# A scan, a routed mixture of experts and a gated block in one kernel: another order of the scan's round, and a tile of its own for the experts' row numbers

## The chip, the cores and the metric

The kernel runs on one core of one Trainium2 chip. The metric is the time of one execution in device microseconds. Before the change the median of three runs is 994.81 us (993.85 to 996.44).

## The reference

Three layers follow each other. The first is linear attention with a decay gate, for 4 batches of 8 heads, 768 steps and 48 columns:

```python
for t in range(S):
    state = f[:, :, t, :, None] * state + np.einsum('bhd,bhe->bhde', k[:, :, t], v[:, :, t])
    y[:, :, t] = np.einsum('bhd,bhde->bhe', q[:, :, t], state)
```

Its output is taken as 3072 tokens of 384 numbers. Each token goes to one of 8 experts, the one of the largest cosine logit; the result is weighted with that expert's softmax probability:

```python
for e in range(E):
    mask = expert_idx == e
    h = np.maximum(x[mask] @ w1[e], 0.0)
    out[mask] = gate_w[mask, None] * (h @ w2[e])
```

with w1[e] of 384x1024 and w2[e] of 1024x384. The last layer is `(x @ w_a) * (x @ w_b) @ w_out`, with 1536 hidden columns. All tensors are fp32. Big products are made as three fp32r matmuls of a high and a low part of each operand.

## The kernel before, in words

The order of every engine's work is written out by hand (`manual_schedule`): each engine runs its instructions in the order in which the program issues them, and waits on semaphores where data or a buffer is not ready. DMAs are issued from the SP queue, in order too, apart from the gathers and scatters, which POOL issues.

**Scan.** The 768 steps are cut into 6 chunks of 128; chunk and batch make 24 groups (`NG`), and the loop over `g` does one group a round. For a group, `scan_b` runs a backward product of the gates on VectorE (tile `Bt`, L188), POOL scales the keys with it (`kt`, L191), and column 0 of `Bt`, the decay over the chunk, goes through a POOL operation into `al_all` (L193). `scan_r` runs the forward scan (`Rt`, L200), `q_scale` scales the queries (L208). `scores` (L244) makes the 128x128 products, evacuated in two halves: VectorE multiplies one by a mask (L261), ScalarE copies the other (L251) and POOL zeroes its upper triangle (L252). `inter` (L268) adds the contribution of the state, `intra` (L275) that of the chunk. `turn_k` and `u_part` make the group's addition to the state, `s_add` (L296) adds it on VectorE, and `s_scale` (L216 on ScalarE for three head pairs, L218 on VectorE for the fourth) multiplies the state by `al_all`. `turn_y` (L302) turns the output into token rows, with the logits beside them. Work is pipelined over rounds: in round `g` the scans are of group `g+2`, scores and masks of `g+1`, outputs of `g`, rows of `g-1`. `warm_up` in each round puts three or one matmul without use on TensorE (L307).

**Routing.** When a set of groups is done (`ROUNDS`), `route` picks experts and positions in small VectorE steps that `tick` deals out between the round's other work, ranks tokens with small matmuls (`rk`), and `scatter_row` lets POOL scatter 128 token rows at a time into `slots` in DRAM (L422), two a round. Each row carries the token's number in column 0 and the gate in column 1.

**Experts.** Expert `e` has 448 places. `rows_load` (L752) reads its 448 rows of 388 numbers from `slots` into the one tile `rows`, 112 partitions of 4 rows; `rows_gate` (L761, ScalarE) multiplies one of the four by the gates, `x_turn` (L781, L784, L785) transposes a third of the columns and splits it. `ids_store` (L769) writes column 0 of `rows`, the token numbers, to a list in DRAM; it has to land before `rows` is loaded anew. The loop runs 64 steps `s`, 8 steps `j` for each expert: `h_part` makes 128 hidden columns (L788 to L790; relu L810 on ScalarE, low part L811 on VectorE), `y_part` of the step before adds them to three outputs (L841), which step 0 of the next expert copies out (L859, L857). `w_more` handles weight pieces of 768 KB with two buffers `raw`: SP loads one (L683), ScalarE makes the high part (L689), POOL and VectorE the low part (L692); a piece of the last layer's weights takes three steps, with four VectorE operations on it (L700 to L710).

In step `j` of expert `e` the program has, after `h_part` and `w_more`: the turn of `e+1` at 3 to 5; at 5 the store of `e+1`'s numbers and the load of `e+2`'s rows; the first gate of `e+2` at 7 and the other three at 0 to 2 of the next expert:

```python
            if 3 <= j <= 5:
                x_turn(e + 1, j - 3)
            elif j == 7:
                rows_gate(e + 2, 0)
            elif j < 3:
                rows_gate(e + 1, j + 1)
            if j == 5 and e + 1 < NE:
                ids_store(e + 1)
                rows_load(e + 2)
            y_part(s - 1)
```

**Last layer.** 6 tiles of 512 tokens by 12 steps of 18 + 12 matmuls, then a scatter to the output.

Of the kernel before, what the change touches and what calls it, by code (L numbers as in the profile page):

```python
# [18 lines left out]
L = 128  # L19
# [15 lines left out]
RB = 8  # L35
# [7 lines left out]
ROUNDS = (7, 15, 19, 21, 23)  # L43
C0 = 2.0 ** -15
NWARM3 = 24
NKEEP = (3, 1)


def build(tc, I, out, dbg=None):
# [50 lines left out]
    def w_hi():  # L100
        n = wstate["hi"]
        if n < wstate["load"]:
            wstate["hi"] += 1
            A.activation(out=w_tile(n)[:, 0], in_=RAW[n], func=ACTF.Copy)

    def w_lo(eng, parts=3):
        n, at = divmod(wstate["lo"], 3)
        if n >= wstate["hi"]:
            return
# [7 lines left out]
    with tc.manual_schedule():  # L117
# [32 lines left out]
        qkf_t = [ob_p.tile([QP, 3, NP, L], F32, name=f"qkf{i}") for i in range(NQ)]  # L150
        u_full = ps_u.tile([128, NP, HP], F32, name="u_ps")
# [31 lines left out]
        def scan_b(g):  # L183
# [3 lines left out]
            Bt = at_p.tile([QP, NP, L + 1], F32, tag="Bt", name="Bt", bufs=2)  # L187
# [5 lines left out]
            G.tensor_scalar(out=al_all[:, g], in0=Bt[:, :, 0], scalar1=1e-30, scalar2=None, op0=ALU.max)  # L193
# [16 lines left out]
        def s_scale(g, a, b):  # L210
# [81 lines left out]
        def s_add(g):  # L292
            if g < 0 or g // B == NCH - 1:
                return
            Sb = S_t[g % B]
            V.tensor_tensor(out=Sb, in0=Sb, in1=u_ps, op=ALU.add)  # L296

        def turn_y(g):
            d = st[g]
            d["x"] = xt = ps_x.tile([128, NP, XW], F32, tag="x", name="x_ps")  # L300
# [13 lines left out]
        def x_sq(g, rd):  # L314
            i, xt = rd["n"], st[g]["x"]
            junk = x_p.tile([128, NP, 2 * D], BF16, tag="junk", name="junk", bufs=1)
# [10 lines left out]
        def x_lg(g, rd):  # L327
            V.tensor_reduce(out=rd["lg"][:, rd["n"]], in_=st[g]["x"][:, :, 2 * D:XW].rearrange("p a e -> p e a"),
                            axis=AX.X, op=ALU.add)

        def x_done(g, rd):
            st.pop(g)
            rd["n"] += 1
# [5 lines left out]
        def route(rd, i0):  # L339
# [6 lines left out]
            def until(k):  # L346
                while it[0] < i0 + k:
                    yield

            yield from until(0.5)  # L350
            nrm = rt("nrm", 1)
            G.tensor_tensor(out=nrm[:, :, 0], in0=ssq, in1=half[:, 0:nb], op=ALU.pow)
            mx = rt("mx", 1)
# [3 lines left out]
            V.tensor_tensor(out=eq, in0=lg, in1=bc(mx), op=ALU.is_ge)  # L357
            z = rt("z")
# [9 lines left out]
            yield from until(1)  # L368
# [9 lines left out]
            V.tensor_scalar(out=nrm, in0=nrm, scalar1=1e-6, scalar2=None, op0=ALU.add)  # L378
            yield
            V.reciprocal(out=nrm, in_=nrm)  # L380
            yield
            V.tensor_tensor(out=z, in0=z, in1=bc(nrm), op=ALU.mult)
            yield from until(1.5)
            A.activation(out=z, in_=z, func=ACTF.Tanh, scale=0.5)
# [10 lines left out]
            new = r_p.tile([128, NE], F32, tag="new", name="new")  # L395
            V.tensor_reduce(out=new, in_=oh.rearrange("p b e -> p e b"), axis=AX.X, op=ALU.add)
            yield
            V.tensor_tensor(out=run, in0=run, in1=new, op=ALU.add)
            yield
            yield from until(2)  # L400
# [13 lines left out]
            for i in range(nb):  # L414
                scaled.append((rd["xb"][:, i], posi[:, i]))

# [12 lines left out]
        def finish(n, upto=1000):  # L429
            it[0] = upto  # L430
            for r in bg[:n]:
# [779 lines left out]
```

## Time and profile before

| | |
|---|---|
| median of the three runs | 994.81 us |
| the profiled execution | 993.71 us, span 991.9 us |
| TensorE, weight load | busy 876.5 us (88%), 757.6 us (76%) |
| VectorE, ScalarE, POOL | busy 438.5, 347.6, 282.1 us |
| mean granted clock of TensorE | 0.927 |
| HBM read and written | 63.79 and 11.90 MB |

The page divides the span of 991.9 us among engines, lines and waits. Its line for TensorE in 40 slices of 24.8 us is `5898888888569578696876999989999999999996`, and that of its granted clock `7898798779798797978999999999999999999999`: 9 is full or nearly so, which of the clock's two levels a stretch has is read in finer windows. The scan lasts to about 180 us, the routing's last rounds and the reading of the first rows to 205, the experts to about 530, the last layer to the end. An engine's idle time counts only where the next one waits for it, so each stage is read by itself.

### The profile page before, as it was taken

To read this page: it belongs to the slowest core of one execution; us is meant where nothing else is said; L and a number is where in the kernel's file an instruction comes from. 1 tells how busy PE (TensorE), PEld (TensorE's weight loads), DVE (VectorE), ACT (ScalarE), POOL (GpSimd) and SP (SyncE) were. 2 spreads that over 40 slices of the span, in tenths; PEclk is the share of its full clock that TensorE was granted. 3 is DMA by queue.
4 is the path that set the end of the run, shared out by engine and by line. 5 is a ranking of instruction groups with operands and counts; after the bars stand their busy time and mean duration, and the time that the engine had idled before them with its cause. 6 is when DMAs were issued, how large, how long until landed. Compare 5 with 4: busy or idle time off the path is not lost.

```text
span 991.9 us, 12790 instructions
## 1 busy us (share of the span) xinstructions
PE 876.5 (88%) x5055; PEld 757.6 (76%) x5060; DVE 438.5 (44%) x719; ACT 347.6 (35%) x631; POOL 282.1 (28%) x267
## 2 busy tenths in 40 slices
PE   5898888569578696876999989999999999999996
PEld 3686776359567595765898878888888888888886
DVE  8899798432324233231467883222222222222222
ACT  3586565323325243242543432122122122122111
POOL 7474766653133151423422322001001001001001
PEclk7898798779798797978999999999999999999999
DMA  9677653244243442434342320000000000000000
GB/s 174 161 185 174 168 141 97 89 120 128 62 124 108 111 128 62 130 120 123 99 94 96 98 95 26 7 1 25 9 1 24 9 1 23 11 1 18 15 1 35
DMA packets 39286, 76.58 MB, mean 77 GB/s; under 512 B 7180, under 2 KB 21348, under 8 KB 39220
## 3 DMA queue, kind: packets, MB, share of 16 engines
q1 hardware_dynamic: 36020, 65.91, 25.5%
q0 software_dynamic: 3072, 9.49, 2.6%
q8 instruction: 42, 0.69, 0.3%
q10 hardware_dynamic: 128, 0.30, 0.1%
q14 instruction: 24, 0.20, 0.1%
HBM read 63.79 MB, written 11.90 MB: 76 GB/s over the span
## 4 chain that ended last, share of the span: by engine, by line
issue 36%; PE 29%; DVE 15%; POOL 8%; DMA 8%; ACT 3%; SPq 0%; POOLq 0%; ACTq 0%; DVEq 0%
DMA raw<-moe_w 4%; PE pa L789 4%; PE pa L790 4%; PE pa L788 4%; PE po L841 4%; POOL w L692 3%; DVE Bt L188 2%; PE pq L963 2%; PE pq L961 2%; PE pq L962 2%; DMA idlist<-rows 2%; DVE Rt L200 2%; DVE gl L950 2%; PE ph L788 1%; PE ph L789 1%
## 5 line engine op out<-in xcount | busy, mean ns | idle before, releaser
L790 PE MATMUL pa<-a,w 128*128 128x512 f32 (+1 forms) x438 | 170.5, 389 | 0.0
L789 PE MATMUL pa<-a,w 128*128 128x512 f32 (+1 forms) x438 | 170.4, 389 | 0.0
L788 PE MATMUL pa<-a,w 128*128 128x512 f32 (+1 forms) x438 | 169.0, 386 | 0.0
L948 DVE TENSOR_TENSOR rows<-rows,pa 128x512 f32<-128x512 f32 (+1 forms) x73 | 49.6, 680 | 242.7 <-PE pa L790 226.6
L841 PE MATMUL po<-hh,w 128*128 128x448 f32 x384 | 100.1, 396 | 55.9 <-ACT hh L810 49.9
L975 POOL DMA_INDIRECT out<-yT,idx x24 | 23.4, 974 | 363.8 <-ACT yT L973 358.3
L841 PEld LDWEIGHTS po<-hh,w 128*128 128x128 f32 x384 | 74.1, 200 | 67.2 <-ACT hh L810 52.6
L811 DVE SCALAR_TENSOR_TENSOR hl<-ph,hh 128x448 fp32r<-128x448 f32 x64 | 39.8, 623 | 164.5 <-ACT hh L810 164.5
L692 POOL TENSOR_TENSOR w<-raw,w 128x512 fp32r<-128x512 f32 x56 | 84.9, 1538 | 60.6 <-ACT w L689 60.6
L944 ACT ACTIVATE rows<-pa 128x512 f32<-128x512 f32 (+1 forms) x73 | 43.1, 591 | 164.7 <-PE pa L790 164.4
L963 PE MATMUL pq<-w,gl 128*128 128x384 f32 x288 | 97.5, 339 | 2.8 <-DVE gl L950 2.7
L961 PE MATMUL pq<-w,gh 128*128 128x384 f32 x288 | 97.0, 337 | 0.8 <-ACT gh L949 0.8
L962 PE MATMUL pq<-w,gh 128*128 128x384 f32 x288 | 96.8, 336 | 0.4 <-POOL w L710 0.4
L949 ACT ACTIVATE gh<-rows 128x512 fp32r<-128x512 f32 (+1 forms) x73 | 45.6, 625 | 143.9 <-DVE rows L948 143.9
L790 PEld LDWEIGHTS pa<-a,w 128*128 128x128 f32 x438 | 82.2, 188 | 16.8
L710 POOL TENSOR_TENSOR w<-raw,w 128x768 fp32r<-128x768 f32 x18 | 33.9, 1882 | 212.1 <-ACT w L709 212.1
L789 PEld LDWEIGHTS pa<-a,w 128*128 128x128 f32 x438 | 82.2, 188 | 15.4
L788 PEld LDWEIGHTS pa<-a,w 128*128 128x128 f32 x438 | 82.3, 188 | 15.1
L950 DVE TENSOR_TENSOR gl<-rows,gh 128x512 fp32r<-128x512 f32 (+1 forms) x73 | 60.0, 822 | 52.1 <-ACT gh L949 49.3
L788 PE MATMUL ph<-a,w 128*128 128x448 f32 x192 | 73.7, 384 | 0.0
L789 PE MATMUL ph<-a,w 128*128 128x448 f32 x192 | 72.8, 379 | 0.0
L790 PE MATMUL ph<-a,w 128*128 128x448 f32 x192 | 72.4, 377 | 0.0
(169 smaller groups left out, 1433.6 us busy)
## 6 DMA issues: line engine op xcount, KB each, us to landing
raw<-moe_w SPq DMA_DIRECT2D x32, 768.0 KB, 4.7
qkf<-qkf SPq DMA_DIRECT2D x44, 288.0 KB, 5.2
rows<-slots SPq DMA_DIRECT2D x7, 679.0 KB, 6.3
vx<-vx SPq DMA_DIRECT2D x24, 192.0 KB, 2.5
raw<-moe_w_a SPq DMA_DIRECT2D x6, 768.0 KB, 7.7
raw<-moe_w_b SPq DMA_DIRECT2D x6, 768.0 KB, 4.6
raw<-moe_w_out SPq DMA_DIRECT2D x6, 768.0 KB, 4.5
slots<-raw SPq DMA_DIRECT2D x8, 291.0 KB
```

Of the source, the lines that this page charges most:

```text
L692: (G if i < NPOOL else V).tensor_tensor(out=wt[:, 1, f], in0=raw[:, f], in1=wt[:, 0, f].bitcast(F32), op=ALU.subtract)
L788: T.matmul(out=out, lhsT=wh, rhs=xh, start=first, stop=False)
L789: T.matmul(out=out, lhsT=wl, rhs=xh, start=False, stop=False)
L790: T.matmul(out=out, lhsT=wh, rhs=xl, start=False, stop=last)
L841: T.matmul(out=OS[e][k], lhsT=w[:, j % 4, k * 128:(k + 1) * 128], rhs=x, start=(j == 0 and w is wh and x is hh), stop=(j == FJ - 1 and x i ...
L944: A.activation(out=ab[:, r], in_=pa, func=ACTF.Copy)
L948: V.tensor_tensor(out=ab[:, r], in0=ab[:, r], in1=pp[1], op=ALU.mult)
L949: A.activation(out=gh[:, r], in_=ab[:, r], func=ACTF.Copy)
L950: V.tensor_tensor(out=gl[:, r], in0=ab[:, r], in1=gh[:, r].bitcast(F32), op=ALU.subtract)
L961: T.matmul(out=q, lhsT=gh[:, c], rhs=wh[:, f % 4], start=(f == 0), stop=False)
L962: T.matmul(out=q, lhsT=gh[:, c], rhs=wl[:, f % 4], start=False, stop=False)
L963: T.matmul(out=q, lhsT=gl[:, c], rhs=wh[:, f % 4], start=False, stop=(f == F2J - 1))
```

## The change

1. **Round of the scan.** `scan_b` and `scores(g+1)` come first, then masks, state, `inter`, `intra`, rows. The logits' sum (`x_lg`) is read a round later. The mask of the POOL half stands ahead of the round's scatters. The matmuls without use are gone from the rounds (3 in each of the first four, 1 in each of the other twenty).
2. **Decays.** `Bt` is kept for the four batches; `s_scale` reads column 0 of it, all four head pairs on ScalarE. The POOL operation of each group is replaced by one ScalarE copy per four groups (`al_keep`). The first addition to a state is a copy, so the states are not zeroed.
3. **Routing.** Sets of 7, 6, 5, 4, 2 groups in place of 8, 8, 4, 2, 2; the steps of `route` are dealt out one by one, and only one point waits for the next round.
4. **Start.** Zeroing of tile 3 of the inputs stands earlier on POOL, two PSUM tiles are zeroed by ScalarE, the expert norms move into rounds 0 and 1.
5. **Weights in the scan.** Loads in rounds 2, 12, 14 and after the last (before 10, 13, 18, 21); high part in thirds; low part of the first two pieces on VectorE.
6. **Experts.** The numbers are copied to a tile `ids` (two of them, VectorE) and stored from there; the load of the next rows follows the copy, at step 4, and the store at 6; the gates come as two and two at steps 0 and 1, the turn at 2 to 4. For expert 0 these are two steps later. `yT` is no longer zeroed.

```diff
-ROUNDS = (7, 15, 19, 21, 23)
+ROUNDS = (6, 12, 17, 21, 23)
-NKEEP = (3, 1)
...
         def scan_b(g):
-            Bt = at_p.tile([QP, NP, L + 1], F32, tag="Bt", name="Bt", bufs=2)
+            Bt = Bt_t[g % B]
...
-            G.tensor_scalar(out=al_all[:, g], in0=Bt[:, :, 0], scalar1=1e-30, scalar2=None, op0=ALU.max)
...
-                for p in range(a, b):
-                    sc = al_all[:HP, g, p:p + 1]
-                    if p < 3:
-                        A.activation(out=Sb[:, p], in_=Sb[:, p], func=ACTF.Copy, scale=sc)
-                    else:
-                        V.tensor_scalar(out=Sb[:, p], in0=Sb[:, p], scalar1=sc, scalar2=None, op0=ALU.mult)
+                for p in range(NP):
+                    A.activation(out=Sb[:, p], in_=Sb[:, p], func=ACTF.Copy, scale=Bt_t[g % B][:HP, p, 0:1])
+        def al_keep(c):
+            A.activation(out=al_all[:, c * B:(c + 1) * B], in_=Bt_all[:, :, :, 0], func=ACTF.Copy)
...
-            V.tensor_tensor(out=Sb, in0=Sb, in1=u_ps, op=ALU.add)
+            if g < B:
+                V.tensor_copy(Sb, u_ps)
+            else:
+                V.tensor_tensor(out=Sb, in0=Sb, in1=u_ps, op=ALU.add)
...
-            if g in (10, 13, 18, 21):
+            if g in (2, 12, 14):
                 w_load()
-            inter(g)
-            intra(g)
             scan_b(g + 2)
-            s_scale(g + 1, 0, NP)
-            tanh(g + 3)
...
-            s_add(g - 1)
-            tick(3)
-            warm_up(NKEEP[g >= B])
             scores(g + 1)
+            tick(g > 5)
+            evac_k(g)
+            tanh(g + 3)
+            mask_a(g + 1)
+            if g > 1:
+                x_lg(g - 2)
+            s_add(g - 1)
+            mask_v(g + 1)
+            gate_f(g + 3)
+            s_scale(g + 2)
...
+            inter(g)
+            intra(g)
             evac_y(g)
...
-            SP.dma_start(out=dst.rearrange("(p j) -> p j", j=4), in_=rows[0:HP, :, 0])
+            SP.dma_start(out=dst.rearrange("(p j) -> p j", j=4), in_=ids[e % 2])
+        def ids_copy(e):
+            if e < NE:
+                V.tensor_copy(ids[e % 2], rows[0:HP, :, 0])
...
-        for k in range(KC):
-            G.memset(yT[k], 0.0)
...
+            late = 2 if e == 0 else 0
+            if late <= j < late + 2:
+                rows_gate(e + 1, 2 * (j - late))
+                rows_gate(e + 1, 2 * (j - late) + 1)
             w_more(s)
-            if 3 <= j <= 5:
-                x_turn(e + 1, j - 3)
...
-            elif j == 7:
-                rows_gate(e + 2, 0)
...
-            if j == 5 and e + 1 < NE:
+            if late + 2 <= j < late + 5:
+                x_turn(e + 1, j - late - 2)
+            if j == late + 4:
+                ids_copy(e + 1)
+                rows_load(e + 2)
+            if j == 6 and e + 1 < NE:
                 ids_store(e + 1)
-                rows_load(e + 2)
```

The order on three engines, at the places of which the prediction speaks. On the SP queue, in the middle of an expert, before (`raw` are weight pieces, `off_i` the address of the list):

```order
L683 DMA raw<-moe_w 128x3x512
L683 DMA raw<-moe_w 128x4x384
L683 DMA raw<-moe_w_b 128x3x512
L767 TENSOR_LOAD off_i
L767 ISA x2
L769 REGISTER_ALU
L769 DMA idlist<-rows 448x1x1
L752 DMA rows<-slots 112x1552
```

and now:

```order
L701 DMA raw<-moe_w 128x4x384
L770 DMA rows<-slots 112x1552
L701 DMA raw<-moe_w_b 128x3x512
L701 DMA raw<-moe_w 128x3x512
L785 TENSOR_LOAD off_i
L785 ISA x2
L787 REGISTER_ALU
L787 DMA idlist<-ids_2285 112x4
```

The load of the rows no longer follows the store of the numbers from the same tile; it stands two weight pieces ahead of it.

On ScalarE, from step 7 of an expert to step 0 of the next, before (`hh` is the relu, `ct` the first operation on a piece of the last layer's weights, `yT` the copy of a finished output):

```order
L810 ACTIVATE hh<-ph 128x448
L761 ACTIVATE rows<-rows 112x384
L810 ACTIVATE hh<-ph 128x448
L700 ACTIVATE ct<-raw 128x768
L761 ACTIVATE rows<-rows 112x384
L850 TENSOR_LOAD off_i
L850 ISA x2
L859 ISA
L859 ACTIVATE yT_2378<-po 128x448
```

and now:

```order
L832 ACTIVATE hh<-ph 128x448 x2
L779 ACTIVATE rows<-rows 112x384 x2
L718 ACTIVATE ct<-raw 128x768
L872 TENSOR_LOAD off_i
L872 ISA x2
L881 ISA
L881 ACTIVATE yT_2280<-po 128x448
```

The gate that waits for new rows stood between the relus of steps 7 and 0; it stands behind the relu of step 0 now.

On POOL, a round of the scan with scatters, before:

```order
L191 TENSOR_TENSOR kt<-qkf_135,Bt 128x512
L193 TENSOR_SCALAR al_all<-Bt 128x4
L324 IOTA xb 128x4
L422 DMA slots<-xb,posi 24576x388 x2
L252 AFFINE_SELECT pm_1235<-pm_1235 128x512
```

and now:

```order
L193 TENSOR_TENSOR kt<-qkf_135,Bt 128x512
L252 AFFINE_SELECT pm_1447<-pm_1447 128x512
L432 DMA slots<-xb,posi 24576x388 x2
L332 IOTA xb 128x4
```

The mask moved ahead of the two scatters, and the operation on `al_all` is gone.

## Rows read from the trace of the kernel before

**Rows 1.** Busy us (count) by stage: PE, PEld, DVE, ACT, POOL; clock, DMA, GB/s.

```profile
26.80:178.50 151.70, 134.30 (x1467) 108.56 (x1470) 130.14 (x224) 95.68 (x232) 98.36 (x111) 0.89 0.59 154
...
258.25:471.44 213.19, 167.64 (x780) 149.76 (x780) 68.75 (x106) 78.23 (x116) 70.02 (x45) 0.86 0.39 109
...
534.73:992.00 457.27, 445.38 (x2158) 391.26 (x2156) 151.92 (x213) 114.12 (x190) 40.28 (x33) 1.00 0.07 23
```

**Rows 2.** Waits of ScalarE in the expert stage: total us, times, longest.

```profile
ACT rows L761 <- DMA rows<-slots: 84.9, 7, 14.9
```

**Rows 3.** Waits of the SP queue at 265 to 480 us.

```profile
SPq L752 <- DMA idlist<-rows: 43.0, 5, 9.4
```

**Rows 4.** Timeline, one stall: start, us, engine, line, operation, [idle before <- releaser].

```profile
334.36 0.35 SPq L752 DMA_DIRECT2D rows<-slots  x1
...
340.40 0.61 ACT L761 ACTIVATE rows<-rows 112x384 f32<-112x384 f32 x1 [13.47 <-DMA rows<-slots]
...
341.35 0.89 ACT L700 ACTIVATE ct<-raw 128x768 f32<-128x768 f32 x1
...
341.50 0.74 PE L841 MATMUL po<-hh,w 128*128 128x448 f32 x1 [7.85 <-ACT hh L810]
...
344.39 0.62 DVE L857 COPY yT<-po 128x448 f32 x1
```

**Rows 5.** ScalarE timeline: copies of two finished experts' outputs.

```profile
471.44 0.98 ACT L859 ACTIVATE yT<-po 128x448 f32 x2
...
502.03 0.98 ACT L859 ACTIVATE yT<-po 128x448 f32 x2 [0.87 <-PE po L841]
```

**Rows 6.** Busy time in the 5 us after that stall.

```profile
345.00:350.00 5.00, 5.00 (x16) 4.46 (x15) 1.97 (x4) 0.19 (x1) 0.00 (x0) 0.56 0.00 0
```

**Rows 7.** TensorE timeline: one round of the scan at full clock.

```profile
50.33 1.13 PE L268 MATMUL y_ps<-qc,S 112*112 112x128 f32 x8
...
51.56 1.08 PE L275 MATMUL y_ps<-pm,vx 128*48 128x128 f32 x16
...
55.98 1.13 PE L268 MATMUL y_ps<-qc,S 112*112 112x128 f32 x8
```

**Rows 8.** TensorE timeline: a round after a late mask.

```profile
114.87 1.94 PE L275 MATMUL y_ps<-pm,vx 128*48 128x128 f32 x14 [2.26 <-POOL pm L252]
```

**Rows 9.** Groups by line at 36 to 180 us: count, busy, mean ns, idle before.

```profile
L307 PE MATMUL wp<-warm,ones 128*128 128x512 bf16 x23 | 9.5, 413 | 0.1
...
L200 DVE TENSOR_TENSOR_SCAN Rt<-F,patr 128x516 f32<-128x516 f32 x20 | 28.6, 1432 | 0.0
...
L218 DVE TENSOR_SCALAR S<-S,al_all 112x112 f32<-112x112 f32 x20 | 21.7, 1084 | 0.0
...
L193 POOL TENSOR_SCALAR al_all<-Bt 128x4 f32<-128x4 f32 x20 | 20.1, 1006 | 1.7
...
L252 POOL TENSOR_SCALAR_AFFINE_SELECT pm<-pm 128x512 f32<-128x512 f32 x21 | 17.2, 820 | 17.2 <-ACT pm L251 17.1
```

**Rows 10.** Timeline of the start.

```profile
18.16 0.63 ACT L173 ACTIVATE F<-qkf 128x512 f32<-128x512 f32 x1 [3.16 <-DMA qkf<-qkf]
...
26.79 1.95 PE L275 MATMUL y_ps<-pm,vx 128*48 128x128 f32 x16 [4.16 <-ACT F L173]
```

**Rows 11.** Timeline between scan and experts.

```profile
198.13 8.96 POOL L869 MEMSET yT<- 128x3520 f32 x3
...
204.22 0.69 DVE L777 TENSOR_TENSOR rows<-rows 112x512 f32<-112x512 f32 x1 [2.45 <-DMA rows<-slots]
...
207.07 1.04 POOL L777 TENSOR_TENSOR rows<-rows 112x512 f32<-112x512 f32 x1
```

**Rows 12.** ScalarE split of a weight piece, undisturbed part of an expert.

```profile
324.22 1.49 ACT L689 ACTIVATE w<-raw 128x1536 fp32r<-128x1536 f32 x1 [0.94 <-DMA raw<-moe_w]
```

**Rows 13.** DMA issues at 265 to 480 us: count, KB each, median us to landing.

```profile
raw<-moe_w SPq DMA_DIRECT2D x20, 768.0 KB, 4.8
...
rows<-slots SPq DMA_DIRECT2D x5, 679.0 KB, 6.3
```

More of the change, by code (lines that the diff above doesn't have):

```diff
@@ L150, in build @@
         qkf_t = [ob_p.tile([QP, 3, NP, L], F32, name=f"qkf{i}") for i in range(NQ)]
+        Bt_all = ob_p.tile([QP, B, NP, L + 1], F32, name="Bt")
+        Bt_t = [Bt_all[:, i] for i in range(B)]
         u_full = ps_u.tile([128, NP, HP], F32, name="u_ps")
@@ L344, in route, with over @@
             prio_b = prio.unsqueeze(1).to_broadcast([128, nb, NE])
-            def until(k):
-                while it[0] < i0 + k:
+            def over():
+                i0 = it[0]
+                while it[0] < i0 + 1:
                     yield
-            yield from until(0.5)
             nrm = rt("nrm", 1)
             G.tensor_tensor(out=nrm[:, :, 0], in0=ssq, in1=half[:, 0:nb], op=ALU.pow)
+            yield
             mx = rt("mx", 1)
@@ L367, in route @@
             V.tensor_tensor(out=oh, in0=eq, in1=bc(m2), op=ALU.is_equal)
-            yield from until(1)
+            yield
+            V.tensor_scalar(out=nrm, in0=nrm, scalar1=1e-6, scalar2=None, op0=ALU.add)
+            yield
+            V.reciprocal(out=nrm, in_=nrm)
+            yield
+            V.tensor_tensor(out=z, in0=z, in1=bc(nrm), op=ALU.mult)
+            yield from over()
             ps = ps_r.tile([128, RB, NE], F32, tag="r", name="rk")[:, 0:nb]
@@ L377, in route @@
                          start=False, stop=(i == nb - 2), skip_group_check=True)
-            V.tensor_scalar(out=nrm, in0=nrm, scalar1=1e-6, scalar2=None, op0=ALU.add)
+            A.activation(out=z, in_=z, func=ACTF.Tanh, scale=0.5)
             yield
[L380 to L384, printed above, removed]
             yield
@@ L394, in route @@
             yield
[L395 to L400, printed above, removed]
             den = rt("den")
@@ L415, in route @@
                 scaled.append((rd["xb"][:, i], posi[:, i]))
+            yield
+            new = r_p.tile([128, NE], F32, tag="new", name="new")
+            V.tensor_reduce(out=new, in_=oh.rearrange("p b e -> p e b"), axis=AX.X, op=ALU.add)
+            yield
+            V.tensor_tensor(out=run, in0=run, in1=new, op=ALU.add)
         scaled = []
@@ L427, in scatter_row, with finish @@
                 scat.append(sc)
-        def finish(n, upto=1000):
-            it[0] = upto
-            for r in bg[:n]:
-                for _ in range(60):
-                    if next(r, "done") == "done":
-                        bg.remove(r)
-                        break
+        def finish():
+            while bg:
+                it[0] += 1
+                tick()
         def flush_rows():
@@ L531, in names @@
                             op=ALU.mult)
+            yield
         setup = names()
-        next(setup)
-        V.memset(run, 0.0)
-        for Sb in S_t:
-            G.memset(Sb, 0.0)
-        G.memset(zero, 0.0)
-        G.affine_select(out=tri, in_=ones, pattern=[[1, 128]], base=0, channel_multiplier=-1,
-                        compare_op=ALU.is_gt, fill=0.0)
-        G.iota(out=prio, pattern=[[-1, NE]], base=NE, channel_multiplier=0,
-               allow_small_or_imprecise_dtypes=True)
-        G.iota(out=base, pattern=[[0, RB], [NT, NE]], base=0, channel_multiplier=0,
-               allow_small_or_imprecise_dtypes=True)
         def zero_fill(i):
@@ L650, in build @@
         idr = sp.tile([24, 128], F32, name="idr")
+        ids = [sp.tile([HP, 4], F32, name=f"ids{i}") for i in range(2)]
         ct = sp.tile([128, 768], I32, name="ct")
```

165 lines of the change are left out of this document (91 added, 74 removed).

## The prediction

> **What bounds the kernel now.** I read the busy time by stage first. The last block takes 457.3 us, TensorE is busy for 445.4 of them at the high level of its clock (granted 1.00, 2.4 GHz), and the change edits nothing there [rows 1]: it stays. What can move lies in the 535 us before.
>
> In the experts the five periods between 258.25 and 471.44 take 213.19 us, 42.6 us each; TensorE is busy for 167.6 of them at a mean grant of 0.86 [rows 1]. The same distance without a stall is there too, because the last expert has no rows to fetch: from the copy of one output at 471.44 to the next at 502.03, 30.6 us [rows 5]. So 12.05 us are lost per expert. The list of waits says to what: ScalarE waits for the rows' DMA seven times, 84.9 us in all, at most 14.9 [rows 2], and the SP queue, before it may issue that DMA, waits for the store of the numbers, 43.0 us in five times [rows 3]. The timeline of one stall shows the chain: the load is issued at 334.36, the gate runs at 340.40 after 13.47 us of idle ScalarE, the relu stands behind that gate, and TensorE's outputs wait 7.85 us for the relu [rows 4]. The other 4.2 us of the 12.05 are the low level of the clock after the idle time: granted 0.56 in 345 to 350 [rows 6].
>
> In the scan 22 rounds, from the second `intra` at 26.79 [rows 10] to the last at 178.5, take 151.7 us, 6.90 each [rows 1]. TensorE alone is the bound in the early rounds: one after the other at the high level is 5.65 us (50.33 to 55.98) [rows 7]. Later rounds lose time when a mask comes late: 2.26 us of waiting for POOL, and then the same product takes 1.94 us instead of 1.08, at the low level [rows 8, 7].
>
> **The change part by part.** The sum goes against the profiled execution, 993.71 us (span 991.9 and 1.8 around it); the median of the runs is 1.1 above it.
>
> *Experts.* The rows' load goes from behind the store of the numbers to ahead of it, one step earlier, and its first gate from step 7 to step 0. The store reads a tile of its own, so nobody waits for it; it now stands behind two weight pieces on SP, with the list needed only at the end. The load stands behind one weight piece that waits for POOL; from step 4 to step 0 there are four steps, 4 x 3.82 = 15.3 us (30.59 / 8), and the DMA needs 6.3 to land [rows 13], so 9 us are left for the queue and for sharing the DMA engines. Six long waits go (the five periods and the one before them): 6 x 12.05 = 72.3 us. What is late next: at step 0 ScalarE does the relu, two gates and then the first operation on the wide weight piece (L700), and VectorE's copy of the middle output (L857) stands behind three operations on that piece. From L700 to the end of that copy it was 344.39 + 0.62 - 341.35 = 3.66 us [rows 4]; a gate and a relu ahead of L700 took 0.95 (340.40 to 341.35), with a second gate some 1.45. So the copy is done 5.1 us after the relu begins, and TensorE comes for the buffer about one step, 3.8 us, after it: a new gap of 1.3 us, six times 7.8. Expert 0 has its gates two steps later and the first load close behind two weight pieces: I allow 2. Sum -72.3 + 7.8 + 2 = -62.5. A gap of 1.3 us may lower the clock or not; no row shows a lone one, so 0 is one end and 6 x 4.2 = 25 us the other; I take 0, since the spells in rows 6 and 8 follow longer waits. The wait that is nearest to becoming a bound is that for weight pieces, 0.94 us in an undisturbed part [rows 12].
>
> *Scan.* TensorE's round without the useless matmul (0.41) [rows 9] is 5.65 - 0.41 = 5.24 us. VectorE had 130.1 / 22 = 5.9 us a round [rows 1] and loses the state's multiplication, 1.08 [rows 9]: 4.8, to which come low parts of weights in a few rounds. ScalarE had 4.35 and takes over a quarter of that state's work; POOL had 4.5 and loses about 0.9 (20.1 us in all) [rows 1, 9]. So the floor is TensorE's 5.24, the ceiling today's 6.90. The masks ahead of the scatters and the scores a round's length before `intra` take away the wait of rows 8. I take 5.65, the pace that was held without routing and scatters, plus a fifth of what separates it from today's, since ranks, gates and two scatters a round stay: 5.9. 22 x 5.9 = 129.8: -22. Ends: 22 x 5.24 = 115.3, -36; and 0.
>
> *Start.* ScalarE waits for the input tile 3 at 18.16, because POOL frees the tile late, and TensorE begins the second `intra` at 26.79 [rows 10]. The zeroing moves ahead of POOL's first key product, the state's zeroing goes, the norms move into rounds. I take -5, less than one round; ends 0 and -8.6, which is all from 18.16 to 26.79.
>
> *Between scan and experts.* POOL's gate of the second third begins at 207.07, as the zeroing of `yT` (8.96 us from 198.13) ends, while VectorE gated the first third at 204.22 [rows 11]: up to 2.85 are free, I take 2. Against it four groups instead of two wait for routing when the scan ends, and their scatters stand ahead of the last ones: ends -3 and +5.
>
> Sum: 993.7 - 62.5 - 22 - 5 - 2 = 902.2; in terms of the median 903.
>
> One rule speaks against the scan's part. Here a scan on VectorE took 1.43 us on average, and POOL's operation on four columns beside it 1.01 [rows 9]; the mask's operation on POOL took 0.82 and now runs early in the round, where the second scan is. The Trainium skill, in "SBUF — State Buffer", section "Who interferes with whom", says that a VectorE instruction with two SBUF inputs and a POOL instruction that reads SBUF exclude each other for the whole instruction. The 1.01 us for four columns agrees with it. By that rule the scan would wait for most of each mask. What this would cost as a mechanism of this kernel is the third rival.
>
> **The rivals.**
> 1. *The clock falls after every new gap in the experts.* For it: the spell after a stall costs 4.2 us. Against: the gap is a sixth of 7.85. 903 + 25 = 928.
> 2. *Weight pieces become the bound.* Per expert five pieces at 4.8 us and the rows at 6.3, one after the other, are 30.3 us [rows 13], as long as the expert itself; the stalls gave them time until now. For it: the 0.94 us of rows 12. Against: two buffers, so loads overlap. With 36 us per expert, 6 x 5.4 = 32: 935.
> 3. *The scan's gain is lost to POOL and VectorE excluding each other.* 22 x 0.82 = 18 us at most, of which I count 0.65 per round, 14: 917. VectorE at 4.8 + 0.65 = 5.45 would still fit under 5.9, which speaks against it.
> 4. *The change does not do what it says*: the rows land after step 0 all the same, behind the weight piece on SP, and ScalarE waits there as it did at step 7. Then 62.5 us come back: 965. Against it stand the 9 us of slack.
> 5. *Slower:* the clock. Without its filling matmuls TensorE could stay at the low level through the scan. A round would be 5.24 x 1.94 / 1.08 = 9.4 us, 22 of them 207, +55; with the falls of rival 1 in the experts -62.5 + 25, nothing gained at the start and -2: 993.7 + 55 - 37.3 - 2 = 1009, 1010 for the median. It decides from about 17 low rounds of 22 (129.8 + 77 f = 151.7 + 39 gives f = 0.79). Against it: at 9.4 us TensorE would be the bound and have no gaps, and the rows of the early rounds show the high level while it is busy without gaps.
>
> **How the numbers follow.** Forecast 0.58 (903); rival 1 0.13; rival 2 0.11; rival 3 0.10; rival 4 0.04; rival 5 0.04. Low end: all parts at their best, 62.5 + 36 + 8.6 + 3 = 110, is 884; I set 882. High end: past rivals 1 and 2 with a few us of scan, 945. Rivals 4 and 5 and a little of 2 stay outside. A measurement of this kernel can tell about 0.3% from no change, 3 us; no case but the last lies near or beyond that on the slow side. Faster 0.95, same 0.01, slower 0.04.
>
> **What would show it.** In the new profile ScalarE should wait for the rows' DMA for next to nothing, the distance between output copies should be 31 to 33 us, and SP should not wait for the list. The rounds of the scan should be 5.6 to 6.2 us, with TensorE's grant near 1 from the third or so, no wait of `intra` for POOL's mask, and the first gate in the experts should not stand behind a zeroing. Wrong would be: gates of ScalarE that wait at step 0, wide weight pieces that land late, rounds at the low level, or a routing tail longer than the 25.7 us from the last `intra` at 178.5 to the first gate at 204.22.

## The result and the profile after

The changed kernel takes 889.63 us, the median of four runs (887.36 to 890.75), against 994.33 us for the kernel before beside it (990.91 to 996.44): a ratio of 0.8947, 95% interval [0.8916, 0.8978]. Its profiled execution took 889.81 us with a span of 888.0; before it was 993.71, so 103.9 us went. The last `intra` of the scan, the first transposes of the experts, and the copies of an expert's output divide both spans alike:

| Stretch | before | after | change | predicted |
|---|---|---|---|---|
| start, to the second `intra` | 26.79 | 22.00 | -4.8 | -5 |
| 22 rounds, to the last `intra` | 151.7 | 120.6 | -31.1 | -22 |
| to the first transposes | 26.6 | 29.1 | +2.5 | -2 |
| to the copy of expert 6's output | 296.9 | 225.5 | -71.4 | -62.5 |
| to the end of the span | 489.9 | 490.8 | +0.9 | 0 |

Busy time of the engines by stage of the changed kernel (PE, PEld, DVE, ACT, POOL, then the granted clock, DMA share, GB/s): the scan's 22 rounds, five periods of the experts, the last block. They answer to [rows 1].

```profile
22.00:142.59 120.59, 111.20 (x1426) 96.96 (x1424) 115.66 (x212) 99.16 (x262) 70.94 (x85) 0.97 0.75 181
213.83:367.24 153.41, 152.84 (x773) 139.28 (x774) 71.93 (x110) 78.61 (x116) 69.81 (x45) 1.00 0.47 150
430.33:888.00 457.67, 446.44 (x2158) 392.60 (x2156) 151.97 (x213) 114.16 (x190) 40.31 (x33) 0.99 0.07 23
```

In the experts TensorE is now busy for 152.84 of 153.41 us at the high level (granted 1.00, 2.4 GHz), where it had 167.6 of 213.2 at 0.86. In the scan VectorE is busy for 96% of the rounds and TensorE for 92%, so there is little left there for either, though a part of VectorE's busy time is waiting for POOL (see POOL and VectorE below). The list of waits from 171 to 430 us (total, times, longest) has this left of the stalls of [rows 2]:

```profile
ACT w L707 <- DMA raw<-moe_w: 8.3, 6, 1.5
ACT rows L779 <- DMA rows<-slots: 4.0, 2, 3.2
PE po L863 <- ACT yT L881: 2.3, 1, 2.3
```

84.9 us in seven waits became 4.0 in two, and SP waits for the list of numbers only once more, 3.0 us at the end. The timeline of ScalarE shows the pace: its copies of an expert's output are 30.80 us apart.

```profile
274.84 0.96 ACT L881 ACTIVATE yT<-po 128x448 f32 x2
305.64 0.96 ACT L881 ACTIVATE yT<-po 128x448 f32 x2
```

The one stretch that got longer is the routing's tail. Its timeline on POOL:

```profile
148.93 0.97 POOL L432 DMA_INDIRECT slots<-xb,posi  x1 [0.30 <-issue]
...
150.00 1.06 POOL L360 TENSOR_TENSOR nrm<-ssq,half 128x4 f32<-128x4 f32 x1
154.02 1.04 POOL L432 DMA_INDIRECT slots<-xb,posi  x1 [2.96 <-DVE new L423]
```

The norm of the second-last set of tokens (150.00) stands behind five scatters that began at 143.78. VectorE waits for it, 3.9 us at most in the list of waits, and then POOL waits 2.96 us for VectorE. From the last `intra` to the first gate of the experts it is 28.2 us (142.59 to 170.82): the prediction named a tail above 25.7 as a sign of being wrong, and in this stretch it was.

### The profile page after: what moved, and what is told of

Read it like the earlier page. It is cut to its first block, busy times and chain, and to the rows that moved or that the text cites. A ratio compares the mean times of both kernels' runs of the same rounds, so it can differ in the third digit from the quotient of the medians.

```text
span 888.0 us, 12718 instructions
## 1 busy us (share of the span) xinstructions
PE 837.8 (94%) x5027; PEld 735.4 (83%) x5028; DVE 426.0 (48%) x710; ACT 352.9 (40%) x663; POOL 245.4 (28%) x230
## 5 line engine op out<-in xcount | busy, mean ns | idle before, releaser
L863 PE MATMUL po<-hh,w 128*128 128x448 f32 x384 | 91.4, 372 | 2.4 <-ACT yT L881 2.3
L832 ACT ACTIVATE hh<-ph 128x448 fp32r<-128x448 f32 x64 | 34.9, 546 | 113.3 <-PE ph L812 113.3
L863 PEld LDWEIGHTS po<-hh,w 128*128 128x128 f32 x384 | 70.4, 188 | 9.2 <-ACT yT L881 2.9
L810 PE MATMUL ph<-a,w 128*128 128x448 f32 x192 | 71.5, 372 | 0.0
L811 PE MATMUL ph<-a,w 128*128 128x448 f32 x192 | 71.1, 371 | 0.0
```

The costliest lines, as they stand in the source:

```text
L810: T.matmul(out=out, lhsT=wh, rhs=xh, start=first, stop=False)
L811: T.matmul(out=out, lhsT=wl, rhs=xh, start=False, stop=False)
L863: T.matmul(out=OS[e][k], lhsT=w[:, j % 4, k * 128:(k + 1) * 128], rhs=x, start=(j == 0 and w is wh and x is hh), stop=(j == FJ - 1 and x i ...
```

## Experiments

Each kernel ran beside the kernel before on the same chip. "The changed kernel" is the one of the diff above. None of the experiments leaves out a part of the computation. Rounds of the scan are compared from the fifth `intra` to the last, because the start varies from one execution to the next: that stretch takes 101.56 to 102.18 us in the changed kernel, e3, e8 and e9, whose rounds are alike up to the last (41.00 to 142.59, 38.91 to 141.09, 39.24 to 140.80, 39.10 to 140.68), and 132.59 in the kernel before (45.92 to 178.51).

**e1: the experts' part alone.** The kernel before with the tile for the numbers and the experts' new order:

```diff
+        ids = [sp.tile([HP, 4], F32, name=f"ids{i}") for i in range(2)]
...
-            SP.dma_start(out=dst.rearrange("(p j) -> p j", j=4), in_=rows[0:HP, :, 0])
+            SP.dma_start(out=dst.rearrange("(p j) -> p j", j=4), in_=ids[e % 2])
...
+            if late <= j < late + 2:
+                rows_gate(e + 1, 2 * (j - late))
+                rows_gate(e + 1, 2 * (j - late) + 1)
...
+            if j == late + 4:
+                ids_copy(e + 1)
+                rows_load(e + 2)
+            if j == 6 and e + 1 < NE:
                 ids_store(e + 1)
-                rows_load(e + 2)
```

> The kernel before with the change's part in the experts alone: the tile for the numbers, the load ahead of the store at step 4, the four gates at steps 0 and 1; the scan, the start and the zeroing of yT stay as before. Theory (the stall was the chain store of the numbers, then load, then gate, and has nothing to do with the scan): the traces before and after differ by 71.4 us from the first transposes (205.12, 171.72) to the copy of expert 6's output (502.03, 397.25), so 994.3 - 71.4 = 923. My prediction's own terms for the experts: 994.3 - 62.5 = 932. Rival (a part of the gain comes from what else the change does, the earlier weights in the scan above all): 935 or more, with waits of ScalarE for weight pieces.

Measured: 919.79 us, ratio 0.9257 [0.9233, 0.9282]. From the first transposes to the copy of expert 6's output its trace has 225.4 us (204.90 to 430.25), as the changed kernel has, 225.5. So the experts' gain comes from the experts' part alone, and the scan's order adds nothing to it that is clear of 2 us. That the two agree to 0.1 us is chance: this kernel still zeroes `yT` and has its first output copy 43.98 us after the first transposes, the changed one after 42.11, and then it takes 181.4 us where the changed one takes 183.4 (the last section has the reason as far as it is known).

**e2: the load early, the gates where they were.** The kernel before with the tile for the numbers, and at step 5:

```diff
             if j == 5 and e + 1 < NE:
-                ids_store(e + 1)
+                ids_copy(e + 1)
                 rows_load(e + 2)
+                ids_store(e + 1)
```

> The kernel before with the tile for the numbers, and the load ahead of the store, but still at step 5, and the gates where they were (step 7, then 0 to 2). Theory: the load is issued when the store was, some 9.8 us earlier (324.5 instead of 334.36), lands 6 us later, and the gate of step 7, for which ScalarE is ready at 326.9, waits 3.6 us instead of 13.47: six stalls cost 6 x 3.6 = 22 and up to 9 of low clock instead of 72: 941 to 953. Rival (the place of the gates is what matters, and the load's place little): over 975.

Measured: 926.71 us, ratio 0.9328 [0.9303, 0.9352], better than the theory had it. The wait at the gate is there, but its price is not. From its list of waits:

```profile
ACT rows L762 <- DMA rows<-slots: 30.8, 7, 6.7
```

ScalarE waits 4.4 us on average, close to the 3.6 expected; the output copies are still only 30.87 us apart (251.76 to 437.00 over six), 0.6 more than the 30.23 of e1 (248.88 to 430.25). So most of a wait of some 4 us at this place is hidden from TensorE, where the theory let it pay in full. Taken in this order, the load's place is worth 66 us of 73 and the gates' place the other 7; e3 takes them in the other order.

**e3: the store first, the gates new.** The changed kernel with the numbers stored from the tile of the rows:

```diff
             if j == late + 4:
-                ids_copy(e + 1)
+                if e + 1 < NE:
+                    ids_store(e + 1)
                 rows_load(e + 2)
...
-            if j == 6 and e + 1 < NE:
-                ids_store(e + 1)
```

> The changed kernel with the numbers stored from the tile of the rows again, so the store stands ahead of the load at step 4; the gates stay at steps 0 and 1. Theory: the load is issued 9.4 us later than in the changed kernel (262.87 + 9.4 = 272.3), lands 6 us later at 278.3, and the gate, for which ScalarE is ready at 273.0, waits 5.3: 6 x 5.3 = 32, with the low clock after it up to 45: 922 to 935. Rival (moving the gates alone takes away the stall, the store is hidden then): within 895. Rival (the store is all of it): 889.6 + 71 = 961.

Measured: 939.77 us, ratio 0.9457 [0.943, 0.9483]: 50 us of the 71 come back, more than the theory had (32 to 45). So moving the gates hides 21 us of the stall and not the store. The timeline of SP, then that of ScalarE, around one gate:

```profile
283.00 0.63 SPq L787 DMA_DIRECT2D idlist<-rows  x1
292.66 0.35 SPq L770 DMA_DIRECT2D rows<-slots  x1
```

```profile
291.72 0.55 ACT L828 ACTIVATE hh<-ph 128x448 fp32r<-128x448 f32 x1 [3.10 <-PE ph L808]
299.17 1.12 ACT L779 ACTIVATE rows<-rows 112x384 f32<-112x384 f32 x2 [6.90 <-DMA rows<-slots]
301.82 0.97 ACT L877 ACTIVATE yT<-po 128x448 f32 x2
```

The load goes out 9.66 us after the store, the rows land 6.5 us later, and the gate waits 6.9, not the 5.3 expected. Here the copies of the outputs stand behind the gates on ScalarE, so TensorE gets the wait: from 296.0 to 301.8 it does nothing, and the granted clock is 0.75 in that window. The periods are 39.2 us on average (221.72 to 417.56 over five), 8.4 more than 30.8, six times: 50. The tile of its own changes the store too: from `rows` it is 448 single numbers and lands in 9.0 us (median, the kernel before), from `ids` it is 112 pieces of four numbers and lands in 3.5 (the changed kernel). No run has the quick store ahead of the load, so what that alone would have given back is not shown.

**e4: the filling matmuls.** The kernel before without them:

```diff
-            warm_up(NKEEP[g >= B])
```

> The kernel before without the useless matmuls in each round of the scan (three in the first four rounds, one later), nothing else. Theory (they cost TensorE 0.41 us each where it is the bound, and hold no clock up): the scan gets 3 to 9 us shorter: 985 to 991. Rival (they hold the clock up, rival 5 of the prediction): the granted clock of the scan falls below the 0.89 of before and the time rises, up to 994 + 55.

Measured: 988.91 us, ratio 0.9946 [0.9927, 0.9965]. They hold no clock up: granted 0.90 over the 22 rounds, 0.89 before. But the theory is hit for a wrong reason. The early rounds, where it put the gain, stay at 5.63 us (40.13 to 62.63 over four). From 40 to 68 us the windows of the kernel before and of this one show why (columns as above):

```profile
40.00:68.00 28.00, 27.68 (x345) 22.68 (x347) 27.42 (x39) 22.48 (x57) 19.69 (x20) 1.00 0.76 197
```

```profile
40.00:68.00 28.00, 26.64 (x340) 22.66 (x340) 27.66 (x41) 22.53 (x57) 19.89 (x20) 1.00 0.83 199
```

VectorE is full in both (27.42 and 27.66 of 28); TensorE is full only before (27.68), and has 26.64 without its useless work. The 2.8 us that the 22 rounds gain (148.95 instead of 151.7) come later.

**e12: the decays alone.** The kernel before with four tiles for the first scan, all four pairs' state scaled on ScalarE from them, and POOL's copy of the decays gone:

```diff
-            G.tensor_scalar(out=al_all[:, g], in0=Bt[:, :, 0], scalar1=1e-30, scalar2=None, op0=ALU.max)
...
+                for p in range(NP):
+                    A.activation(out=Sb[:, p], in_=Sb[:, p], func=ACTF.Copy, scale=Bt_t[g % B][:HP, p, 0:1])
```

> The kernel before with the decays read from the scan's own tiles alone: four of these tiles, all four head pairs of the state scaled on ScalarE, POOL's copy of the decays gone (one copy by ScalarE for four rounds instead). Theory (the early rounds ran at VectorE's pace, 5.63 us, of which this takes an operation of up to 1.26): early rounds of 5.1 to 5.3, eight of them, and some of the late masks, since POOL loses 20 us: 980 to 989. Rival (TensorE bounds the early rounds, with its useless matmul): they stay at 5.6, 990 or more. Rival (this part is most of the scan's gain): 962 to 975.

Measured: 980.14 us, ratio 0.9866 [0.9835, 0.9898]; the 22 rounds take 138.3 us, 13.4 less, at a granted clock of 0.96 instead of 0.89. The early rounds come to 5.47 us (45.56 to 67.45 over four), not 5.1, and now TensorE is the full one:

```profile
40.00:68.00 28.00, 27.95 (x353) 23.09 (x352) 25.67 (x36) 23.86 (x65) 9.54 (x15) 1.00 0.79 199
```

With e4 this settles the early rounds: two bounds lay side by side, VectorE at 5.63 us and TensorE with its useless matmul at 5.47. The changed kernel takes away both and runs at 5.11 (41.00 to 51.21 over two). But the early rounds are less than 1 us of the 13.4. 6.0 come from the three rounds with ranks (9.76, 9.75 and 6.42 us before; 6.70, 7.12 and 6.08 here), where TensorE's waits for the ranks' input fell from 5.3 to 2.2 us. Its waits for POOL's mask did not fall (5.7 us in five, 5.9 in four before), though POOL lost 19 us of work.

**e6: the fourth pair back on VectorE.** The changed kernel with:

```diff
+                    if p < 3:
                         A.activation(out=Sb[:, p], in_=Sb[:, p], func=ACTF.Copy, scale=sc)
+                    else:
+                        V.tensor_scalar(out=Sb[:, p], in0=Sb[:, p], scalar1=sc, scalar2=None, op0=ALU.mult)
```

> The changed kernel with the fourth head pair of the state scaled on VectorE again (20 operations; the factor is read from the scan as the other three's). Theory (VectorE is as full as TensorE in the scan, 115.9 of 121 us): each operation costs its own duration, 0.37 us if nothing runs on POOL beside it and up to 1.26 if it has to wait for POOL's operation: 20 x 0.37 to 1.26 = +7 to +25, 897 to 915. Rival (TensorE alone bounds the rounds, as the prediction had it for the early ones): no change, within 3 us of 889.6.

Measured: 890.53 us, ratio 0.8963 [0.8921, 0.9004], which can't be told from the changed kernel: the theory missed, and the time is the rival's. Its trace is finer: from the fifth `intra` to the last it takes 104.0 us (41.41 to 145.41), 2.4 more. The early rounds stay at 5.11 (41.41 to 51.62 over two), so the multiplication by itself was not what held them at VectorE's pace; its length there was. The 20 operations cost far less here than before. The line's instructions in the kernel before, then in e6 (ns, shortest/median/longest):

```profile
L218 DVE TENSOR_SCALAR S<-S,al_all x20: 371/1260/1275, 41.6 to 172.9; 112x112 f32<-112x112 f32 x20
```

```profile
L219 DVE TENSOR_SCALAR S<-S,Bt x20: 269/580/826, 31.7 to 137.5; 112x112 f32<-112x112 f32 x20
```

**e5: the scatters ahead of the masks.** The changed kernel with the round's scatters moved up from behind `turn_y`:

```diff
             tanh(g + 3)
+            for _ in range(2 if g < NG - 2 else 6):
+                scatter_row()
             mask_a(g + 1)
```

> The changed kernel with the round's two scatters issued on POOL ahead of the mask again, nothing else. Theory now (scores come a whole round ahead of intra, so the mask has room): two scatters take 2 x 1.3 = 2.6 us, the mask of the next round would be done some 3 us later and is needed some 4 us after its usual end: same to 3 us slower, 889 to 893. Rival (the prediction's reading, late masks behind scatters are what the scan lost): intra waits for the mask again in 9 rounds with scatters, 2 us each and the low clock behind it: 900 to 915.

Measured: 889.12 us, ratio 0.895 [0.8912, 0.8987]: nothing that the time can tell, as the theory had it. In the trace the stretch from the fifth `intra` to the last takes 103.0 us (40.02 to 142.99), 1.4 more, and TensorE waits 1.3 us for POOL's mask. Once the scores come a round ahead, the mask's place behind or ahead of the scatters is worth 1.4 us. The place in the order of before is another question, and this run doesn't ask it.

**e7: scores and masks behind `intra`.** The changed kernel with these three moved down, the routing's operations left where they are:

```diff
             intra(g)
+            scores(g + 1)
             evac_y(g)
+            mask_a(g + 1)
+            mask_v(g + 1)
```

> The changed kernel with the next round's scores and its two masks behind intra again, as before the change. Theory (the order of the round is worth little by itself while VectorE and TensorE are both full; the early rounds of the kernel before ran at VectorE's pace): some rounds wait for the mask on POOL or on VectorE by up to 1 us: 0 to +15, 890 to 905. Rival (the order is what took the clock's falls away): PE waits for pm return, the granted clock of the scan falls to the 0.89 of before: +15 to +30.

Measured: 893.52 us, ratio 0.8992 [0.8948, 0.9037]; the last `intra` is at 145.95 instead of 142.59. One wait of 2.7 us for the ranks' input is new, and the granted clock from 100 to 143 us is 0.92, not 1.00. The time alone leaves it open whether this is slower; from the fifth `intra` to the last the trace shows 4.1 us (40.25 to 145.95, 105.7). TensorE's waits for POOL's mask come to 1.3 us in two.

**e11: the routing ahead of the scores too.** The kernel of e7, and:

```diff
             V.tensor_tensor(out=oh, in0=eq, in1=bc(m2), op=ALU.is_equal)
+            ps = ps_r.tile([128, RB, NE], F32, tag="r", name="rk")[:, 0:nb]
+            T.matmul(out=ps, lhsT=tri, rhs=oh, start=True, stop=False, skip_group_check=True)
...
+            tick(3 if g < 19 else 6)
             scores(g + 1)
```

> The kernel of e7 (scores and masks behind intra) with the routing's operations of a round ahead of the scores too, and the ranks' matmuls straight behind the operation on VectorE that they read, in the same round, as before the change. Theory (what cost the routing rounds of the kernel before was one chain: ranks wait for VectorE, scores stand behind them, the masks behind the scores, intra behind the masks, and the clock falls): TensorE waits 2 us or more for oh in four sets, intra waits for pm again, each with low clock after it: 893.5 + 4 x (2 to 4) = 901 to 910, clock of the scan's second half near 0.9. Rival (the loss was VectorE and POOL being full, which stays mended here): within 4 us of 893.5.

Measured: 908.66 us, ratio 0.9144 [0.9116, 0.9172], 15 more than e7 (its profiled execution took 903.34). TensorE's waits from the second `intra` (25) to the last (157.3):

```profile
PE rk L379 <- DVE oh L377: 10.6, 3, 4.5
PE y_ps L275 <- POOL pm L252: 2.1, 3, 1.4
```

The last `intra` is at 157.35, and the clock of the rounds is 0.92. The three rounds with ranks take 10.01, 12.88 and 11.75 us, where most others take 5.1 to 5.5; from the fifth `intra` to the last it is 116.1 us (41.21 to 157.35), 14.6 more than in the changed kernel. The same chain stands in the kernel before, in the round from 74.07 to 83.83 us, which takes 9.76 instead of 5.63:

```profile
78.11 0.22 DVE L367 TENSOR_TENSOR oh<-eq,m 128x64 bf16<-128x64 f32 x1
78.39 0.19 PE L370 MATMUL rk<-oh,tri 128*128 128x64 bf16 x1 [2.17 <-DVE oh L367]
79.17 1.62 PE L244 MATMUL pp<-qc,kt 64*128 64x128 f32 x16
```

The ranks wait for VectorE at the head of TensorE's queue, the scores stand behind them and take 1.62 us (1.16 a round earlier, at 70.74), and the masks and the next `intra` follow late. So the order does carry a large part of the scan's gain, and ranks ahead of scores are one pair that counts. This run exaggerates their price: its waits for ranks are twice those of the kernel before (10.6 against 5.3 us, three each). Nor does it put the scatters ahead of the masks, as the kernel before has them.

**e8: the zeroing of `yT` back.** The changed kernel with, ahead of the experts:

```diff
+        for k in range(KC):
+            G.memset(yT[k], 0.0)
```

> The changed kernel with the zeroing of the three output tiles on POOL between scan and experts again. Theory: POOL is idle for 6.94 us until the rows land at 171.83 and the zeroing takes 8.96, so the gate of the second third begins 2 us later and the first expert with it: +1 to +3, 891 to 893. Rival (worth nothing, since TensorE's second set of transposes waits for something else): within 1 us.

Measured: 888.43 us, ratio 0.8947 [0.8907, 0.8987]: too small for the time. In the trace the second set of transposes begins 32.29 us after the last `intra` (140.80 to 173.09), against 30.35 (142.59 to 172.94): +1.9, as the theory priced it. The scan's end, 1.8 us earlier, and the pace of the experts, 30.44 us here and 30.80 there, took it back in this execution.

**e9: the norm ahead of the five scatters.** The changed kernel with the route's first operations of the second-last set issued early in the last round:

```diff
                 x_lg(g - 2)
+            if g == NG - 1:
+                tick(2)
```

> The changed kernel with the norm of the second-last set of tokens issued on POOL ahead of the five scatters of the set before it. Theory (the routing's tail is POOL's: VectorE waited 3.91 us for this norm and POOL then 2.96 for VectorE): the stretch from the last intra to the first transposes, 29.1 us in the changed kernel, gets 3 us shorter, 886 to 887 against 889.6. Rival (the tail hangs on VectorE's chain of small operations): within 1 us.

Measured: 885.13 us, ratio 0.8912 [0.8888, 0.8936]. POOL no longer pauses:

```profile
141.66 1.15 POOL L360 TENSOR_TENSOR nrm<-ssq,half 128x4 f32<-128x4 f32 x1
143.01 1.04 POOL L432 DMA_INDIRECT slots<-xb,posi  x1 [0.20 <-DVE nrm L379]
...
149.49 0.99 POOL L432 DMA_INDIRECT slots<-xb,posi  x1 [0.17 <-issue]
```

From the last `intra` to the first transposes it takes 26.35 us (140.68 to 167.03) instead of 29.13: 2.8 less, so that part of the tail was POOL's.

**e10: four sets.** The changed kernel with the last two sets in one, whose norm comes ahead of nine scatters:

```diff
-ROUNDS = (6, 12, 17, 21, 23)
+ROUNDS = (6, 12, 17, 23)
...
-            for _ in range(2 if g < NG - 2 else 6):
+            for _ in range(2):
                 scatter_row()
...
         finish()
-        scatter_row()
-        scatter_row()
```

> The changed kernel with four sets of tokens instead of five (the last two become one of six), two scatters a round to the end, and the last set's norm ahead of nine scatters. Theory (the tail is POOL's): its last scatter ends 2 to 4 us earlier, 886 to 888. Rival (the last set's ranks and gates for six tokens per partition, which start only after the last round, take longer on VectorE than POOL has scatters to do in the meantime): 889 to 893.

Measured: 886.64 us, ratio 0.8925 [0.8902, 0.8948]. The same stretch takes 26.32 us (141.49 to 167.81), as in e9. The two versions can't be told apart, and either is the fastest here; that they beat the changed kernel is shown by this stretch, while the intervals of the ratios still overlap.

## Why the prediction was right, and where its steps were not

The time (889.6) lies in the range (882 to 945), 13 us under the forecast of 903, and the mechanisms that it named acted, in the experts with the size that it read, in the scan beside two that it missed. The low end counted the experts at their forecast (62.5) and not at the 72.3 that it read; they gave 71.4, so that the time stayed above 882 is in part owed to parts that gave less than their ends. Step by step:

- **Experts, -62.5 against -71.4.** The six stalls were worth 6 x 12.05 = 72.3, as read. What failed is "a new gap of 1.3 us, six times 7.8". It is zero. The step had TensorE come for the buffer that VectorE's copy of the middle output frees. The timeline of one step 0 shows otherwise:

```profile
275.30 0.37 PE L812 MATMUL ph<-a,w 128*128 128x448 f32 x1
276.12 1.40 PE L863 MATMUL po<-hh,w 128*128 128x448 f32 x6
277.09 0.61 DVE L879 COPY yT<-po 128x448 f32 x1
277.36 0.78 PE L863 MATMUL po<-hl,w 128*128 128x448 f32 x3
```

  VectorE's copy is late as predicted (277.09 to 277.70), but the six products for all three new outputs begin at 276.12 and run through. The first products of all three outputs have begun before VectorE's copy does, so none of the three writes the buffer that it reads. Of four buffers one was free, and the other two are those that ScalarE has copied out by then (274.84 to 275.80). The 2 us for expert 0 were about right: one wait of ScalarE of 3.2, of which TensorE saw 2.3.
- **The slack of the load.** "9 us are left" was less: the load stands on SP behind three weight pieces and goes out at 262.87, its gate is at 273.04, and landing takes some 6 us, so 4 are left. That there is slack, and that some more lateness is hidden, decided; e2 shows the second.
- **Scan, -22 against -31.1.** Two steps failed. First, "TensorE alone is the bound in the early rounds": taking out its useless matmul alone changes nothing there (e4), taking VectorE's operation out, with POOL's, gives 5.47 (e12); the changed kernel, without all three, has 5.11. In the kernel before VectorE is as full there as TensorE (27.42 and 27.68 of 28 us). The floor of 5.24 came near by accident. Second, for the later rounds the step took one cause, masks behind scatters, from [rows 8], and left a fifth of the loss standing "since ranks, gates and two scatters a round stay". The cause was there, but it was one of three. TensorE's waits in the kernel before (36 to 178.5 us) are:

```profile
PE y_ps L275 <- POOL pm L252: 5.9, 4, 2.3
PE rk L370 <- DVE oh L367: 5.3, 3, 2.2
PE y_ps L275 <- DVE pm L261: 4.2, 5, 1.3
```

  In each of the four rounds of the first line the two scatters stand right ahead of the mask on POOL; ahead of the wait of [rows 8] it is

```profile
109.50 0.60 ACT L251 ACTIVATE pm<-pp 128x512 f32<-128x512 f32 x1 [0.38 <-PE pp L244]
...
111.21 1.27 POOL L422 DMA_INDIRECT slots<-xb,posi  x1 [0.17 <-issue]
...
112.79 1.36 POOL L422 DMA_INDIRECT slots<-xb,posi  x1 [0.30 <-issue]
...
114.16 0.66 POOL L252 TENSOR_SCALAR_AFFINE_SELECT pm<-pm 128x512 f32<-128x512 f32 x1
```

  With the scores behind `intra`, the waits for POOL's mask are 5.9 and 5.7 us where the scatters are ahead of it (before, e12) and 1.3 and 2.1 where they are behind (e7, e11); with the scores a round ahead the place is worth 1.4 (e5). What the step had wrong is that ranks and gates stay: behind the scores and a round after their input, the ranks no longer make TensorE wait in the rounds, and the mean granted clock from the third `intra` (31.11) to the last is 1.00. From the fifth `intra` to the last, the pieces are 13.3 (e12: 45.56 to 164.86), 2.4 (e4: 45.72 to 175.94) and 14.6 (e11 against the changed kernel), 30.2 of 31.0. They were taken from both ends and overlap: e12 shortens the waits for ranks too, and e11 exaggerates them. That they add up this closely is luck, and how the later rounds' gain divides between ranks and scatters in the order of before is not shown.
- **Start, -5 against -4.8.** Right, but in this execution part of it was only moved: the third `intra` is at 31.11 against 33.94, 2.8 earlier, because TensorE waits 2.5 us for `pick`, whose norms now come in the rounds. Other executions of the same start differ: in e3, e8 and e9 the second `intra` is at 23.63 to 23.71, later, and the third at 28.31 to 28.68, earlier, with a wait for `pick` of 0.4 to 0.6 us in e8 and e9. So the start and the 22 rounds of the table are uncertain by 2 to 4 us against each other.
- **Between scan and experts, -2 against +2.5.** The 2 us for the zeroing are there (e8: 1.9). The prediction put the scatters of four groups into the upper end, +5, and nothing for them into the value. What was late next it did not name: the second-last set's norm behind five scatters on POOL, 2.8 us (e9). The text's bound of +5 held it, the value taken did not.
- **Rivals.** The clock after new gaps fell away with the gaps. Weight pieces are late six times, by 1.5 us at most, and hide. That the change does not do what it says would have looked like e3, 50 us back. Rival 5 falls with e4.
- **POOL and VectorE excluding each other.** The third rival priced this at 14 us. The second scan went from 1.45 us on average to 1.52 and `qc` from 0.69 to 0.81; 21 of each make 4 us, of which the first scan gave back 2 (1.34 to 1.22). But waiting of this kind was there in the kernel before, in the operation that the change removed: L218 takes 0.37 us at its shortest and 1.26 in most rounds, where it starts with POOL's `kt` and ends with it.

```profile
76.17 1.25 DVE L218 TENSOR_SCALAR S<-S,al_all 112x112 f32<-112x112 f32 x1
76.18 1.17 POOL L191 TENSOR_TENSOR kt<-qkf,Bt 128x512 f32<-128x512 f32 x1 [0.63 <-issue]
```

  By the Trainium skill, "SBUF — State Buffer", section "Who interferes with whom", a `tensor_scalar` may take both of VectorE's ports and then one of the two engines blocks until the other is done; the durations agree with that, no run isolates it. So the rule was held against the change, while the kernel before was paying for it: of the 21.7 us of [rows 9] some 14 (20 x (1.08 - 0.37)) were, by this estimate, waiting.

## What to carry to other kernels

When a stall is a chain of DMAs, look for the transfer that stands in it only because of the tile it reads: a copy of a few bytes into a tile of its own, with the load moved ahead of the store, took away 66 us in e2. Before you name the bound of a stage, put all engines' busy time beside each other: two bounds 3% apart hide each other, and removing either one alone shows nothing or little. A line's shortest and median duration can tell whether a full engine works or waits. What waits at the head of an engine's queue delays all that is behind it, so put the long chain (scores, masks) ahead of what waits for another engine (ranks) or can wait (scatters), and read the next queue that the moved work joins, as the norm behind five scatters shows.

## What was not expected of the hardware

The experts' period has two values, 30.44 us and 30.80, at a granted clock of 1.00 throughout and with the same work: 30.44 in e1, e5 to e9 and e11, 30.80 in the changed kernel and in e10; e9, e10 and e11 ran on one chip. From the second output copy to that of expert 6 it makes 153.2 us in the changed kernel and 151.4 in e8, so a difference of 2 us between kernels is read from stretches of the trace, not from the total. The last block doesn't follow it: 457.7 and 457.2 us with the long period (the changed kernel, e10), 457.1 to 458.4 with the short. What sets it is open.

A wait of ScalarE is worth very different amounts by its place: 4.4 us on average cost TensorE 0.6 a period in e2, where the gate stood behind the relu of step 7, and 7 us cost 8.4 in e3, where the output copies stood behind the gate.
